# Router logits of the second expert layer computed by VectorE in some slots of the first expert layer

## The chip, the cores and the metric

One core of one Trainium2 chip runs the program. The metric is the device time of one execution in microseconds (us); the profile comes from one more execution, recorded by the hardware profiler.

## The reference

Three stages follow one another on 3,072 tokens of 512 numbers (fp32).

```python
x = attention(q, k, v, lam)                      # decayed linear attention, blocks of 64
# first expert layer: 8 experts, each token goes to one
e = argmax(x @ w_gate + modality_bias[modality_id])
x1 = gate_w * (relu(x @ w1[e]) @ w2[e])          # w1 512x1024, w2 1024x512
# second expert layer: a skip score and a second router decide
do = x1 @ w_skip > 0                             # w_skip: 512
logits = x1 @ w_gate2                            # w_gate2: 512 x 8
e2 = argmax(logits)                              # gate = 1 / sum(exp(logits - max))
out = x1 + do * gate2 * (relu(x1 @ w1b[e2]) @ w2b[e2])
```

The inputs are drawn with a fixed seed. For them the first layer's experts 0 to 7 get 0, 0, 0, 1319, 0, 253, 1494 and 6 tokens.

## The kernel before

**Slots.** Each expert layer works through slots of up to 256 tokens of one expert. A table kernel (`table`) on VectorE orders the experts from the fullest on and cuts their tokens into slots. For the inputs above the first layer has 14 slots: expert 6 in slots 0 to 5, expert 7 in slot 6 (6 tokens), expert 3 in slots 7 to 12 (39 tokens in the last), expert 5 in slot 13. A slot with at most 128 tokens is run as a half slot (`layer1_half`), by a flag `full` that every engine loads into a register one slot ahead; the flag comes from row 3 of `ei`. A slot that begins a new expert splits that expert's weights into a high and a low part on ScalarE and VectorE: `split_w2` at the slot's start, `split_w1` already in the layer 2 of the slot before (`split_next`).

**One slot** (`slot`) runs: layer 1 (eight column blocks f of w1, 12 matmuls of 256 columns each, hidden values to `p1`; after each second f ScalarE writes relu to `hh`, VectorE the rest to `hl`), then `trans_x` (eight transposes of the next slot's rows into `xth` and `xtl`, double-buffered by slot parity), then layer 2 for the two halves of the tokens (24 matmuls of 512 columns each into `p2[j]`). ScalarE scales the result into `x2r[parity][j]`; it is written to `xs2` and to the output.

**The router of the second layer** works one slot behind, in the layer 1 of the next slot (`router`): `tr` after f = 1 (eight TensorE transposes of `x2r`, copied by ScalarE to `x2t`), `la` after f = 3 (the products with `wgp`, 9 columns padded to 32, into `plg`), `rk` after f = 4 on VectorE (a transpose of `plg` into `L`, then argmax, the skip mask and the running counts `rs`), and `rb` in layer 2 (j = 0) after its fourth step: two small matmuls for the row numbers, eight small VectorE instructions, an Exp on ScalarE and two scatters by GpSimd into the second layer's table.

**Order.** The order of each engine's instructions is the order in which they are written out (`manual_schedule`). Inside an If, every engine that has work in it branches on its own register. All VectorE instructions count on one semaphore, and so do TensorE's and ScalarE's; an instruction that overwrites what the one before on its engine wrote waits for that one.

Of the kernel before, what the change touches and what calls it, by code (L numbers as in the profile page):

```python
# [9 lines left out]
F32 = mybir.dt.float32  # L10
# [4 lines left out]
AF = mybir.ActivationFunctionType  # L15
ALU = mybir.AluOpType
# [18 lines left out]
@with_exitstack  # L35
def body(ctx: ExitStack, tc: tile.TileContext, qkv, cpk, w1, w2, out, dbg=None):
    nc = tc.nc
# [150 lines left out]
    def choose(which, n):  # L188
        t = rt.tile([P, E], F32, tag="t_p", name="t_p")
        g = rt.tile([P, E], F32, tag="t_g", name="t_g")  # L190
        mx = rt.tile([P, 1], F32, tag="t_mx", name="t_mx")
        mp = rt.tile([P, 1], F32, tag="t_mp", name="t_mp")
        b = eb[:, which]
# [13 lines left out]
    def table(which):  # L207
        n = count(pcnt[which])
        x = rt.tile([P, KT, E], F32, tag="t_x", name="t_x")
        nr = rt.tile([P, E], F32, tag="t_nr", name="t_nr")  # L210
# [23 lines left out]

        u = rt.tile([P, E], F32, tag="t_u", name="t_u")
        y = rt.tile([P, KT], F32, tag="t_y", name="t_y")
        base = rt.tile([P, KT], F32, tag="t_b", name="t_b")
        nc.vector.scalar_tensor_tensor(out=u, in0=cc[:, 0:E], scalar=-float(T), in1=erow, op0=ALU.mult, op1=ALU.add)
# [5 lines left out]
        pick(eid, y)  # L244
        nx = rt.tile([P, E, E], F32, tag="t_nx", name="t_nx")
        nc.vector.tensor_tensor(out=nx, in0=bc(c1.unsqueeze(2), [P, E, E]), in1=bc(c1.unsqueeze(1), [P, E, E]), op=ALU.is_ge)
        nxe = rt.tile([P, E], F32, tag="t_nxe", name="t_nxe")
        nc.vector.tensor_reduce(out=nxe, in_=nx, axis=AX.X, op=ALU.add)
        w = rt.tile([P, KT], F32, tag="t_w", name="t_w")
        hx = rt.tile([P, KT], F32, tag="t_hx", name="t_hx")  # L250
        g2 = rt.tile([P, E], F32, tag="t_g2", name="t_g2")
        g3 = rt.tile([P, E], F32, tag="t_g3", name="t_g3")
        nc.vector.tensor_scalar(out=g2, in0=nxe, scalar1=estar, scalar2=None, op0=ALU.add)
# [5 lines left out]
        fin = ge[:, :, E - 1]  # L259
        nw = rt.tile([P, KT - 1], F32, tag="t_nw", name="t_nw")  # L260
        if which:
# [10 lines left out]
        nc.vector.scalar_tensor_tensor(out=u, in0=cc[:, 0:E], scalar=float(T), in1=nr, op0=ALU.mult, op1=ALU.add)  # L272
        rem = rt.tile([P, KT], F32, tag="t_r", name="t_r")
# [48 lines left out]
    def is_full(ap):  # L322
        return nc.values_load(ap, engines=FE, min_val=0, max_val=1,
                              skip_runtime_bounds_check_because="it is a comparison's result")

# [335 lines left out]
    def router(ix, kk=None):  # L661
# [38 lines left out]

        return tr, la, rk, rb

    def layer1(kk, steps, lead=False):
        xh, xl = xth[kk % 2], xtl[kk % 2]
        for f in range(8):
            pt = p1[(f // 2) % 3]
# [16 lines left out]
    def layer1_half(kk, steps):  # L723
        fs_ = [steps[f] for f in sorted(steps)]
        xh, xl = xth[kk % 2], xtl[kk % 2]
        for g in range(2):
            o = p1[g].rearrange("p a t -> p (a t)")
            fs = slice(g * 512, (g + 1) * 512)
            for c in range(4):
                nc.tensor.matmul(o, xh[:, c, 0:P], w1h[c][:, fs], start=(c == 0), stop=False)  # L730
                nc.tensor.matmul(o, xl[:, c, 0:P], w1h[c][:, fs], start=False, stop=False)
                nc.tensor.matmul(o, xh[:, c, 0:P], w1l[c][:, fs], start=False, stop=(c == 3))
            nc.scalar.activation(out=hrow[g], in_=o.rearrange("p (a f) -> p a f", f=P), func=AF.Relu)
            if g < len(fs_):
                fs_[g]()
# [41 lines left out]
    def first1():  # L777
# [35 lines left out]
    def first2():  # L813
        la, rk, rb = router(itl)[1:]

# [22 lines left out]
    def slots(which):  # L838
# [10 lines left out]
        def slot(kk, fl, full):  # L849
# [22 lines left out]
            if which == 0:  # L872
                tr, la, rk, rb = router(it[(kk - 1) % 6], kk - 1)
# [4 lines left out]
            with tc.If(full > 0, preferred_fallthrough_block=True) as c:  # L878
                layer1(kk, steps)
            with c.Else():  # L880
                layer1_half(kk, {} if which else {1: steps[1], 3: lambda: (la(), rk())})
# [93 lines left out]
```

## Time and profile before

| | |
|---|---|
| times of three runs | 704.35, 704.1, 699.21 us; median 704.1 |
| profiled execution, its own time | 700.19 us |
| its span | 698.5 us |
| TensorE busy in the span | 670.4 us (96%) |
| VectorE busy | 361.3 us (52%) |
| mean granted clock of TensorE | 0.996 |

The span is what the trace covers; the other 1.7 us of the profiled execution lie around it. Times in the rows are us from the span's start, unless marked ns. L713 is line 713 of the kernel.

### The profile page before, as it was taken

To read this page: it belongs to the slowest core of one execution; us is meant where nothing else is said; L and a number is where in the kernel's file an instruction comes from. 1 tells how busy PE (TensorE), PEld (TensorE's weight loads), DVE (VectorE), ACT (ScalarE), POOL (GpSimd) and SP (SyncE) were. 2 spreads that over 40 slices of the span, in tenths; PEclk is the share of its full clock that TensorE was granted. 3 is DMA by queue.
4 is the path that set the end of the run, shared out by engine and by line. 5 is a ranking of instruction groups with operands and counts; after the bars stand their busy time and mean duration, and the time that the engine had idled before them with its cause. 6 is when DMAs were issued, how large, how long until landed. Compare 5 with 4: busy or idle time off the path is not lost. (4 is left out here: it accounts for less than half of the span.)

```text
span 698.5 us, 16309 instructions
## 1 busy us (share of the span) xinstructions
PE 670.4 (96%) x5628; PEld 596.3 (85%) x5628; DVE 361.3 (52%) x920; ACT 262.4 (38%) x462; POOL 222.5 (32%) x287
## 2 busy tenths in 40 slices
PE   6999999899999999999999999999999999999994
PEld 5889988779988988799889887987998899887993
DVE  5656676663223315862233236868227575758650
ACT  2444434522222224832222226532115543556430
POOL 4356556252231132432311313234121222113221
PEclk9999999999999999999999999999999999999998
DMA  8778767647321232993211201631815558557500
GB/s 279 228 207 225 212 208 212 213 117 279 123 89 56 68 122 60 306 328 125 80 38 43 92 33 63 207 138 49 298 61 178 185 207 281 189 184 275 176 17 29
DMA packets 60504, 109.65 MB, mean 157 GB/s; under 512 B 18656, under 2 KB 18784, under 8 KB 60368
## 3 DMA queue, kind: packets, MB, share of 16 engines
q1 hardware_dynamic: 48400, 86.65, 38.0%
q0 software_dynamic: 9744, 20.47, 8.7%
q10 hardware_dynamic: 2224, 0.93, 0.6%
q8 instruction: 60, 0.98, 0.6%
q14 instruction: 76, 0.62, 0.3%
HBM read 84.08 MB, written 30.06 MB: 163 GB/s over the span
## 5 line engine op out<-in xcount | busy, mean ns | idle before, releaser
L713 PE MATMUL p<-xth,w1h 128*128 128x256 f32 x672 | 190.1, 283 | 4.2 <-ACTq L887 1.8
L713 PE MATMUL p<-xth,w1l 128*128 128x256 f32 x672 | 187.0, 278 | 0.0
L713 PE MATMUL p<-xtl,w1h 128*128 128x256 f32 x672 | 186.8, 279 | 0.0
L719 DVE SCALAR_TENSOR_TENSOR hl<-p,hh 128x512 fp32r<-128x512 f32 x84 | 57.7, 690 | 177.8 <-ACT hh L718 176.1
L752 PE MATMUL p<-w2h,hh 128*128 128x512 f32 x360 | 144.3, 401 | 0.0
L754 PE MATMUL p<-w2h,hl 128*128 128x512 f32 x360 | 141.5, 393 | 0.6 <-DVE hl L743 0.6
L753 PE MATMUL p<-w2l,hh 128*128 128x512 f32 x360 | 141.3, 392 | 0.4 <-DVE w2l L311 0.2
L713 PEld LDWEIGHTS p<-xth,w1h 128*128 128x128 f32 x672 | 126.2, 188 | 7.7 <-ACTq L887 2.3
L713 PEld LDWEIGHTS p<-xtl,w1h 128*128 128x128 f32 x672 | 126.2, 188 | 1.1 <-DVEq L772 0.5
L713 PEld LDWEIGHTS p<-xth,w1l 128*128 128x128 f32 x672 | 127.1, 189 | 0.0
L718 ACT ACTIVATE hh<-p 128x512 fp32r<-128x512 f32 x84 | 50.2, 598 | 184.1 <-PE p L713 182.0
L161 POOL DMA_INDIRECT out_dram<-x2r,it x43 | 50.4, 1171 | 199.7 <-DVE x2r L765 97.6
L754 PEld LDWEIGHTS p<-w2h,hl 128*128 128x128 f32 x360 | 67.6, 188 | 16.3 <-DVE hl L743 1.5
L753 PEld LDWEIGHTS p<-w2l,hh 128*128 128x128 f32 x360 | 67.7, 188 | 15.6 <-DVE w2l L311 2.4
L752 PEld LDWEIGHTS p<-w2h,hh 128*128 128x128 f32 x360 | 67.7, 188 | 13.0
L161 POOL DMA_INDIRECT tab<-pk,rows x28 | 32.0, 1143 | 143.7 <-issue 120.8
L165 POOL DMA_INDIRECT xg<-xs,it x54 | 60.2, 1115 | 28.7 <-issue 18.8
L311 DVE TENSOR_TENSOR w2l<-raw,w2h 128x1024 fp32r<-128x1024 f32 x48 | 55.9, 1219 | 6.8 <-ACT w2h L310 5.9
L762 ACT ACTIVATE x2r<-p,it 128x512 f32<-128x512 f32 x26 | 17.9, 688 | 106.8 <-PE p L754 92.3
L310 ACT CAST w2h<-raw 128x1024 fp32r<-128x1024 f32 x48 | 49.1, 1048 | 22.2 <-issue 12.5
L305 DVE TENSOR_TENSOR w1l<-raw,w1h 128x512 fp32r<-128x512 f32 x88 | 54.0, 686 | 0.9 <-issue 0.4
L304 ACT CAST w1h<-raw 128x512 fp32r<-128x512 f32 x88 | 47.0, 637 | 0.0
(214 smaller groups left out, 798.2 us busy)
## 6 DMA issues: line engine op xcount, KB each, us to landing
raw<-in_w_dram SPq DMA_DIRECT2D x96, 512.0 KB, 5.2
kq<-in_qkv_dram SPq DMA_DIRECT2D x48, 256.0 KB, 3.4
xs<-x2r SPq DMA_DIRECT2D x28, 256.0 KB, 2.6
v<-in_qkv_dram SPq DMA_DIRECT2D x24, 256.0 KB
xs<-xr SPq DMA_DIRECT2D x24, 256.0 KB, 6.1
xs<-xgm SPq DMA_DIRECT2D x7, 512.0 KB
xg<-xs,it POOLq DMA_INDIRECT x54, 4.7
tab<-tini ACTq DMA_DIRECT2D x2, 416.0 KB
```

The lines of the kernel that those rows point to most:

```text
L161: nc.gpsimd.indirect_dma_start(out=dst, out_offset=bass.IndirectOffsetOnAxis(ap=idx, axis=0), in_=rows, in_offset=None, bounds_check=dst.s ...
L165: return nc.gpsimd.indirect_dma_start(out=rows, out_offset=None, in_=src, in_offset=bass.IndirectOffsetOnAxis(ap=idx, axis=0), bounds_chec ...
L304: nc.scalar.copy(out=w1h[c][:, s], in_=raw1[:, c, s])
L305: nc.vector.tensor_tensor(out=w1l[c][:, s], in0=raw1[:, c, s], in1=f32(w1h[c][:, s]), op=ALU.subtract)
L310: nc.scalar.copy(out=w2h[c], in_=r)
L311: nc.vector.tensor_tensor(out=w2l[c], in0=r, in1=f32(w2h[c]), op=ALU.subtract)
L713: nc.tensor.matmul(o, w[c][:, fs], x[:, c, :], start=(n == 0), stop=(n == 11))
L718: nc.scalar.activation(out=a, in_=pt, func=AF.Relu)
L719: nc.vector.scalar_tensor_tensor(out=b, in0=pt, scalar=0.0, in1=f32(a), op0=ALU.max, op1=ALU.subtract)
L752: nc.tensor.matmul(p2[j], a, w2h[g][:, i], start=(n == 0), stop=False)
L753: nc.tensor.matmul(p2[j], a, w2l[g][:, i], start=False, stop=False)
L754: nc.tensor.matmul(p2[j], b, w2h[g][:, i], start=False, stop=(n == 7))
```

## The change

In slots 2 to 10 of the first layer, layer 1 is cut into three Ifs (f = 0 and 1; f = 2 and 3; f = 4 to 7). The flag of the first layer becomes 2 where the slot is full and neither it nor the next one begins a new expert. Where it is 2, VectorE computes the 9 logits for the 2 times 128 tokens of the slot before, with 18 instructions `tensor_tensor_reduce`: each multiplies `x2r[..][j]` (128x512) by one row of `wgb` and sums along the row into one column of `L`. The products, which nobody reads, go to `xtl` of the slot before. `wgb` holds the 9 weight rows on every partition; SP loads it once, in `first1`, between the loads of w1 and w2. 11 of the 18 stand ahead of layer 1, 3 ahead of f = 2 and 4 behind f = 3. Where the flag is less, `tr`, `la` and the transpose of `plg` (`turn`) stay, at the same places of layer 1. In all slots 2 to 10 `rk` stands behind the last `hl`, the `hl` of f = 4 to 7 is written in two instructions of 256 columns, and `rb` stands after the seventh step of layer 2 (j = 0), and so behind `split_next`. Slots 1 and 11 to 13 keep the old order. The small tiles of `table` and `choose` get one buffer in place of two.

```diff
-        nc.vector.tensor_scalar(out=ei_[:, 3 * KT:4 * KT], in0=rem, scalar1=float(P), scalar2=None, op0=ALU.is_gt)
+        if which:
+            nc.vector.tensor_scalar(out=ei_[:, 3 * KT:4 * KT], in0=rem, scalar1=float(P), scalar2=None, op0=ALU.is_gt)
+        else:
+            nc.vector.tensor_tensor(out=w[:, 0:KT - 2], in0=nw[:, 0:KT - 2], in1=nw[:, 1:KT - 1], op=ALU.max)
+            nc.vector.tensor_scalar(out=w[:, 0:KT - 2], in0=w[:, 0:KT - 2], scalar1=-1.0, scalar2=2.0, op0=ALU.mult, op1=ALU.add)
+            nc.vector.scalar_tensor_tensor(out=ei_[:, 3 * KT + 1:4 * KT - 1], in0=rem[:, 1:KT - 1], scalar=float(P),
+                                           in1=w[:, 0:KT - 2], op0=ALU.is_gt, op1=ALU.mult)
...
+    wgb = hp.tile([P, E + 1, D], F32, name="wgb")
...
+        def lg(j, es):
+            for e in es:
+                nc.vector.tensor_tensor_reduce(
+                    out=xtl[kk % 2][:, :, j * P:(j + 1) * P], in0=x2r[kk % 2][j].rearrange("p (c t) -> p c t", t=P),
+                    in1=wgb[:, e].rearrange("p (c t) -> p c t", t=P), scale=1.0, scalar=0.0, op0=ALU.mult, op1=ALU.add,
+                    accum_out=box["L"][:, j, e:e + 1])
+
+        def turn():
+            if "L" not in box:
+                box["L"] = rt.tile([P, 2, 32], F32, tag="L2", name="L2", bufs=1)
+            nc.vector.transpose(out=box["L"].rearrange("p j e -> p (j e)"), in_=plg)
+
         def rk():
-            L = rt.tile([P, 2, 32], F32, tag="L2", name="L2")
-            nc.vector.transpose(out=L.rearrange("p j e -> p (j e)"), in_=plg)
+            if "L" not in box:
+                turn()
+            L = box.pop("L")
...
-                nc.vector.scalar_tensor_tensor(out=b, in0=pt, scalar=0.0, in1=f32(a), op0=ALU.max, op1=ALU.subtract)
+                for q in range(parts):
+                    q_ = slice(q * 2 // parts, (q + 1) * 2 // parts)
+                    nc.vector.scalar_tensor_tensor(out=b[:, q_], in0=pt[:, q_], scalar=0.0, in1=f32(a[:, q_]), op0=ALU.max, op1=ALU.subtract)
...
         behind(ld_w1(e), got)
+        nc.sync.dma_start(out=wgb, in_=bc(wgr.unsqueeze(0), [P, E + 1, D]))
         ld_w2(e)
...
+            if which == 0 and 2 <= kk <= 10:
+                box["L"] = rt.tile([P, 2, 32], F32, tag="L2", name="L2", bufs=1)
+                own = nc.values_load(ei[0][0:1, 3 * KT + kk:3 * KT + kk + 1], engines=(ET.DVE,), min_val=0, max_val=2,
+                                     skip_runtime_bounds_check_because="it comes from comparisons' results")
+                with tc.If(own > 1):
+                    lg(0, range(E + 1))
+                    lg(1, range(0, 2))
+                with tc.If(full > 0, preferred_fallthrough_block=True) as c:
+                    layer1(kk, {}, (0, 1))
+                with c.Else():
+                    half_rows(kk, 0)
+                with tc.If(full > 1, preferred_fallthrough_block=True) as c:
+                    lg(1, range(2, 5))
+                    layer1(kk, {}, (2, 3))
+                    lg(1, range(5, E + 1))
+                with c.Else():
+                    with tc.If(full > 0, preferred_fallthrough_block=True) as c2:
+                        steps[1]()
+                        layer1(kk, {}, (2, 3))
+                        la()
+                        turn()
+                    with c2.Else():
+                        steps[1]()
+                        half_rows(kk, 1)
+                        la()
+                        turn()
+                with tc.If(full > 0, preferred_fallthrough_block=True) as c:
+                    layer1(kk, {}, range(4, 8), parts=2)
+                with c.Else():
+                    half_cols()
+                rk()
+            else:
+                with tc.If(full > 0, preferred_fallthrough_block=True) as c:
+                    layer1(kk, steps)
+                with c.Else():
+                    layer1_half(kk, {} if which else {1: steps[1], 3: lambda: (la(), rk())})
             trans_x(which, kk + 1, ptr)
             hooks = {1: ahead, 5: lambda: split_next(which, kk + 1, fl2)}
             if which == 0:
-                hooks[3] = rb
+                hooks[6 if 2 <= kk <= 10 else 3] = rb
```

`half_rows(kk, g)` and `half_cols()` are the two loops of the old `layer1_half`, cut out as functions.

## Rows read from the trace of the kernel before

**Rows 1.** The page's part 1: busy us of each engine, share, instructions.

```profile
PE 670.4 (96%) x5628; PEld 596.3 (85%) x5628; DVE 361.3 (52%) x920; ACT 262.4 (38%) x462; POOL 222.5 (32%) x287
```

**Rows 2.** Who waited for whom: us in total, times, longest us.

```profile
ACT hh L718 <- PE p L713: 182.0, 78, 13.2
DVE hl L719 <- ACT hh L718: 176.1, 64, 10.6
```

**Rows 3.** Timeline of TensorE in slot 2: start us, us, line, operation, tiles.

```profile
178.90 0.28 PE L713 MATMUL p<-xth,w1h 128*128 128x256 f32 x1
...
181.53 0.28 PE L713 MATMUL p<-xth,w1l 128*128 128x256 f32 x1
...
182.64 0.28 PE L713 MATMUL p<-xtl,w1h 128*128 128x256 f32 x1
...
185.23 0.28 PE L713 MATMUL p<-xth,w1l 128*128 128x256 f32 x1
...
186.25 0.28 PE L713 MATMUL p<-xtl,w1h 128*128 128x256 f32 x1
...
191.47 0.28 PE L713 MATMUL p<-xth,w1l 128*128 128x256 f32 x1
...
195.22 0.18 PE L137 MATMUL pmi<-oh,tri 128*128 128x16 bf16 x1
...
203.63 0.28 PE L713 MATMUL p<-xth,w1h 128*128 128x256 f32 x1
```

**Rows 4.** Timeline of VectorE in slot 2.

```profile
186.95 0.13 DVE L681 CAST idf<-it 128x2 f32<-128x2 int32 x1
...
188.63 0.36 DVE L133 TENSOR_TENSOR rs<-rs,oh 128x8 bf16<-128x8 bf16 x2
...
192.42 0.69 DVE L719 SCALAR_TENSOR_TENSOR hl<-p,hh 128x512 fp32r<-128x512 f32 x1 [1.97 <-ACT hh L718]
...
195.47 0.17 DVE L141 COPY rs<-rs 128x8 bf16<-128x8 bf16 x1 [1.16 <-PE pmi L138]
...
196.50 0.17 DVE L158 RECIPROCAL pk<-s 128x2 f32<-128x2 f32 x1
```

**Rows 5.** Branch instructions of layer 1's If (L878), 194 to 206 us: ns, start.

```profile
L878 DVEq COMPARE_BRANCH  x1: 50/50/50, 198.2 to 198.2; - x1
```

**Rows 6.** Register loads (L323) of VectorE in the same stretch: ns, start.

```profile
L323 DVEq TENSOR_LOAD <-ei x1: 311/311/311, 197.8 to 197.8; - x1
```

**Rows 7.** Groups by form: busy us, mean ns, idle before.

```profile
L305 DVE TENSOR_TENSOR w1l<-raw,w1h 128x512 fp32r<-128x512 f32 x88 | 54.0, 686 | 0.9 <-issue 0.4 <-ACT w1h L304 0.3
...
L133 DVE TENSOR_TENSOR rs<-rs,oh 128x8 bf16<-128x8 bf16 x52 | 8.5, 163 | 1.8
...
L743 DVE TENSOR_TENSOR hl<-p,hh 128x256 fp32r<-128x256 f32 x12 | 4.3, 417 | 1.5 <-ACT hh L740 1.5
...
L455 DVE TENSOR_TENSOR_SCAN dm<-lad,diag 128x512 f32<-128x512 f32 x2 | 2.4, 1224 | 0.1
...
L233 DVE TENSOR_REDUCE t_r<-t_x 128x24 f32<-128x192 f32 x2 | 0.7, 354 | 0.1
```

**Rows 8.** Timeline of VectorE in slot 5: a run of splits.

```profile
271.08 4.91 DVE L305 TENSOR_TENSOR w1l<-raw,w1h 128x512 fp32r<-128x512 f32 x8 [0.16 <-issue]
```

**Rows 9.** Branch instructions of L878, 182 to 194 us (end of slot 2's layer 1).

```profile
L878 PEldq COMPARE_BRANCH  x1: 305/305/305, 189.6 to 189.6; - x1
```

**Rows 10.** Timeline of TensorE where half slot 6 skips its second half.

```profile
292.71 0.40 PE L754 MATMUL p<-w2h,hl 128*128 128x512 f32 x1
293.84 0.38 PE L713 MATMUL p<-xth,w1h 128*128 128x256 f32 x1 [0.73 <-ACTq L887]
```

**Rows 11.** A stretch of slot 1: busy us by engine, clock, DMA share, GB/s.

```profile
155.00:160.00 5.00, 5.00 (x45) 5.00 (x44) 0.69 (x1) 1.56 (x3) 0.23 (x1) 1.00 0.96 323
```

**Rows 12.** Timeline of SP's queue behind the load of w1.

```profile
167.95 0.40 SPq L335 DMA_DIRECT2D it<-tab  x1
```

**Rows 13.** Timeline of GpSimd in slot 2.

```profile
197.47 1.09 POOL L161 DMA_INDIRECT tab<-pk,rows  x1 [13.39 <-issue]
```

More of the change, by code (lines that the diff above doesn't have):

```diff
@@ L35, in body @@
 @with_exitstack
-def body(ctx: ExitStack, tc: tile.TileContext, qkv, cpk, w1, w2, out, dbg=None):
+def body(ctx: ExitStack, tc: tile.TileContext, qkv, cpk, w1, w2, wgr, out, dbg=None):
     nc = tc.nc
@@ L188, in choose @@
     def choose(which, n):
[L189 to L192, printed above, removed]
+        t = rt.tile([P, E], F32, tag="t_p", name="t_p", bufs=1)
+        g = rt.tile([P, E], F32, tag="t_g", name="t_g", bufs=1)
+        mx = rt.tile([P, 1], F32, tag="t_mx", name="t_mx", bufs=1)
+        mp = rt.tile([P, 1], F32, tag="t_mp", name="t_mp", bufs=1)
         b = eb[:, which]
@@ L233, in pick @@
             nc.vector.tensor_reduce(out=out, in_=x, axis=AX.X, op=ALU.add)
-        u = rt.tile([P, E], F32, tag="t_u", name="t_u")
-        y = rt.tile([P, KT], F32, tag="t_y", name="t_y")
-        base = rt.tile([P, KT], F32, tag="t_b", name="t_b")
+        u = rt.tile([P, E], F32, tag="t_u", name="t_u", bufs=1)
+        y = rt.tile([P, KT], F32, tag="t_y", name="t_y", bufs=1)
+        base = rt.tile([P, KT], F32, tag="t_b", name="t_b", bufs=1)
         nc.vector.scalar_tensor_tensor(out=u, in0=cc[:, 0:E], scalar=-float(T), in1=erow, op0=ALU.mult, op1=ALU.add)
@@ L244, in table @@
         pick(eid, y)
-        nx = rt.tile([P, E, E], F32, tag="t_nx", name="t_nx")
+        nx = rt.tile([P, E, E], F32, tag="t_nx", name="t_nx", bufs=1)
         nc.vector.tensor_tensor(out=nx, in0=bc(c1.unsqueeze(2), [P, E, E]), in1=bc(c1.unsqueeze(1), [P, E, E]), op=ALU.is_ge)
-        nxe = rt.tile([P, E], F32, tag="t_nxe", name="t_nxe")
+        nxe = rt.tile([P, E], F32, tag="t_nxe", name="t_nxe", bufs=1)
         nc.vector.tensor_reduce(out=nxe, in_=nx, axis=AX.X, op=ALU.add)
[L249 to L252, printed above, removed]
+        w = rt.tile([P, KT], F32, tag="t_w", name="t_w", bufs=1)
+        hx = rt.tile([P, KT], F32, tag="t_hx", name="t_hx", bufs=1)
+        g2 = rt.tile([P, E], F32, tag="t_g2", name="t_g2", bufs=1)
+        g3 = rt.tile([P, E], F32, tag="t_g3", name="t_g3", bufs=1)
         nc.vector.tensor_scalar(out=g2, in0=nxe, scalar1=estar, scalar2=None, op0=ALU.add)
@@ L259, in table @@
         fin = ge[:, :, E - 1]
-        nw = rt.tile([P, KT - 1], F32, tag="t_nw", name="t_nw")
+        nw = rt.tile([P, KT - 1], F32, tag="t_nw", name="t_nw", bufs=1)
         if which:
@@ L322, in is_full @@
     def is_full(ap):
-        return nc.values_load(ap, engines=FE, min_val=0, max_val=1,
-                              skip_runtime_bounds_check_because="it is a comparison's result")
+        return nc.values_load(ap, engines=FE, min_val=0, max_val=2,
+                              skip_runtime_bounds_check_because="it comes from comparisons' results")
     def XG(which, kk):
@@ L699, in rb, with layer1 @@
                 scatter(tabv[1][j], pk[:, j, :], rows[:, j:j + 1])
-        return tr, la, rk, rb
-    def layer1(kk, steps, lead=False):
+        return tr, la, rk, rb, lg, turn
+    def layer1(kk, steps, fr=range(8), lead=False, parts=1):
         xh, xl = xth[kk % 2], xtl[kk % 2]
-        for f in range(8):
+        for f in fr:
             pt = p1[(f // 2) % 3]
@@ L718, in layer1, with half_rows, half_cols @@
                 nc.scalar.activation(out=a, in_=pt, func=AF.Relu)
-                nc.vector.scalar_tensor_tensor(out=b, in0=pt, scalar=0.0, in1=f32(a), op0=ALU.max, op1=ALU.subtract)
+                for q in range(parts):
+                    q_ = slice(q * 2 // parts, (q + 1) * 2 // parts)
+                    nc.vector.scalar_tensor_tensor(out=b[:, q_], in0=pt[:, q_], scalar=0.0, in1=f32(a[:, q_]), op0=ALU.max, op1=ALU.subtract)
             if f in steps:
                 steps[f]()
-    def layer1_half(kk, steps):
-        fs_ = [steps[f] for f in sorted(steps)]
+    def half_rows(kk, g):
         xh, xl = xth[kk % 2], xtl[kk % 2]
[L726 to L735, printed above, removed]
+        o = p1[g].rearrange("p a t -> p (a t)")
+        fs = slice(g * 512, (g + 1) * 512)
+        for c in range(4):
+            nc.tensor.matmul(o, xh[:, c, 0:P], w1h[c][:, fs], start=(c == 0), stop=False)
+            nc.tensor.matmul(o, xl[:, c, 0:P], w1h[c][:, fs], start=False, stop=False)
+            nc.tensor.matmul(o, xh[:, c, 0:P], w1l[c][:, fs], start=False, stop=(c == 3))
+        nc.scalar.activation(out=hrow[g], in_=o.rearrange("p (a f) -> p a f", f=P), func=AF.Relu)
+    def half_cols():
         for g in range(2):
@@ L743, in layer1_half @@
                 nc.vector.tensor_tensor(out=hl[g][:, as_, 0:P], in0=pt[:, as_], in1=f32(hh[g][:, as_, 0:P]), op=ALU.subtract)
+    def layer1_half(kk, steps):
+        fs_ = [steps[f] for f in sorted(steps)]
+        for g in range(2):
+            half_rows(kk, g)
+            if g < len(fs_):
+                fs_[g]()
+        half_cols()
         for st_ in fs_[2:]:
@@ L813, in first2 @@
     def first2():
-        la, rk, rb = router(itl)[1:]
+        la, rk, rb = router(itl)[1:4]
         tb = table(1)
@@ L876, in slot @@
             full2 = is_full(ei[which][0:1, 3 * KT + kk + 1:3 * KT + kk + 2])
[L878 to L881, printed above, removed]
+            if which == 0 and 2 <= kk <= 10:
+                box["L"] = rt.tile([P, 2, 32], F32, tag="L2", name="L2", bufs=1)
+                own = nc.values_load(ei[0][0:1, 3 * KT + kk:3 * KT + kk + 1], engines=(ET.DVE,), min_val=0, max_val=2,
+                                     skip_runtime_bounds_check_because="it comes from comparisons' results")
+                with tc.If(own > 1):
[23 more added lines that the diff above has]
+                with c.Else():
+                    half_cols()
+                rk()
[4 more added lines that the diff above has]
+                    layer1_half(kk, {} if which else {1: steps[1], 3: lambda: (la(), rk())})
             trans_x(which, kk + 1, ptr)
@@ L920, in body @@
         dbg(nc, locals())
-_INS = ["qkv", "cpk", "w1", "w2"]
+_INS = ["qkv", "cpk", "w1", "w2", "wgr"]
 _OUTS = [((3072, 512), "float32")]
@@ L957 @@
         _np.ascontiguousarray(ids).view(_np.float32)], axis=1)
+    inputs["wgr"] = _np.concatenate([_np.asarray(inputs[n]).reshape(hd, -1) for n in ("moe2_w_gate", "moe2_w_skip")], axis=1).T
     inputs["w1"] = _np.concatenate([inputs["moe_w1"], inputs["moe2_w1"]], axis=0)
```

20 lines of the change are left out of this document (10 added, 10 removed).

## The prediction

> **What bounds the kernel now.** I read the busy times first: TensorE works in 96% of the span, VectorE in 52% [rows 1]. Then the list of waits: the longest are ScalarE waiting for TensorE's hidden values and VectorE waiting for ScalarE behind it, 182 and 176 us [rows 2]. So the other engines wait for TensorE, not it for them. Then the timeline of TensorE through one slot: it issues without a gap from 178.90 to the next slot's first matmul at 203.63, one slot in 24.73 us [rows 3]. In that stage anything taken off TensorE shortens the program one for one, as long as nothing else becomes late. Read VectorE's timeline of the same slot for what it has left: some 10 us of small work, the rest idle [rows 2, 4].
>
> **In how many slots.** The flag is 2 where the slot is full, is not the first of its expert, and the next slot is not either. With the slots that the token counts give (expert 6 in 0 to 5, expert 7 in 6, expert 3 in 7 to 12), within 2 to 10 these are 2, 3, 4 and 8, 9, 10: six slots, in two runs of three. Slots 5, 6 and 7 take the other branches.
>
> **What is removed, per slot.** From the last layer-1 matmul ahead of the transposes to the second behind them it is 182.64 - 181.53 = 1.11 us; two steps in the undisturbed layer 1 take 2 x 0.115 = 0.23 (from 186.25 to 191.47 there are 46 steps: 0.1135 each; from 182.64 to 185.23 22: 0.118). So `tr` costs TensorE 1.11 - 0.23 = 0.88. In the same way `la`: 186.25 - 185.23 - 0.23 = 0.79 [rows 3]. Together 1.67 us; six slots: **10.0 us**. Two copies of ScalarE and VectorE's transpose go too; neither is waited for here.
>
> **What VectorE gets, per slot.** 18 sums. No row shows this instruction, so let s be the time from one start to the next, and see how large s may be. VectorE's queue of one slot, in the new order: 18 s; two `hl` of 512 columns at 0.69 + 0.03 [rows 4]; two pairs of 256 columns, at 0.417 each and overlapped [rows 7], 0.80 a pair; `rk` without the transpose, from 186.95 to the end of L133 at 188.99, 2.04 [rows 4]. That is 18 s + 5.1. It begins after `rb`: its first VectorE instruction starts 0.25 behind the small matmul (195.22 to 195.47), the last ends 1.20 later (196.67) [rows 3, 4]; then the branches and register loads until layer 1's branch at 198.25 take 1.6 [rows 5], and the load of `own` with its branch I put at 0.4 more, for such a load takes 0.311 [rows 6] and a branch 0.050 [rows 5]. So the sums start 3.45 us behind the matmul of `rb`, and `rk` has to be done when the next slot's `rb` comes, one slot of 24.73 - 1.67 = 23.06 later, for TensorE stands still there until `oh` is ready. 18 s + 5.1 + 3.45 <= 23.06 gives **s <= 0.806**. Each 0.01 above costs 0.18 us a slot, and at s = 0.90 the 1.67 are gone. All other needs are looser: `p1` of f = 0 is wanted again at f = 6, layer 2 wants the last `hl` 20 matmuls in.
>
> **Which s.** The bounds are 0.60 below (eight subtractions of the same 128x512, both operands in SBUF, in 4.91: 0.60 from start to start [rows 8]) and 1.26 above (the scan over two streams of 512 takes 1224 ns [rows 7], and 0.04 for a wait). The multiplication alone takes 686 ns, and a reduction of 192 elements 354, as much above its length as the others have: summing goes at the same rate there [rows 7]. All sums of one j write the same part of `xtl`, so each waits for the one before; such a wait adds 0.04 (L133 twice in 0.36 at 0.163 each [rows 4, 7]): 0.73. If the sum is written out by a small instruction of its own, overlapped like the subtractions, it is 0.60 + 0.16 + 0.04 = 0.80. I take 0.77, nearest to the plain 686 ns row, and so no loss; but the margin is 0.04. [...]
>
> **The rest.** The three Ifs: TensorE's own branch at the end of layer 1 runs at 189.6, while the matmuls last until 191.6 [rows 3, 9]. The sequencer is 2 us ahead, and a branch takes 0.3, so two more are hidden; uncovered they would cost some 0.4 each. That nothing stands still at today's block ends: behind 191.47 the transposes and layer 2 follow (TensorE has no gap until 195.22) though VectorE's `hl` of the block only starts at 192.42 [rows 3, 4]. `rb` moves behind nine more matmuls of 0.23: GpSimd's scatter starts 2.1 us later; GpSimd has waited 13.39 us for it [rows 13], and what is queued behind (the output scatters, the gathers for the slot after next) has a slot to spare. In slots 5 and 6 `rb` also stands behind `split_next`, 4.91 us of VectorE [rows 8] and as much of ScalarE (for the Exp); `split_w2` comes 1.4 later in slot 7, and layer 2 reads it 13 us on. Nothing. In half slot 6 `hl` no longer waits behind `rk`: at most 0.4 gained. `wgb` is 128 x 18,432 bytes, 2.36 MB, behind w1 on SP's queue. At the 323 GB/s of that stretch it takes 7.3 us; the load of w2 and the DMA of the table at 167.95 come that much later [rows 11, 12]. w2 is split five slots later. The first sums of slot 2 need `wgb` at about 175; if it comes later than that, one slot loses up to some 3 us, which I put at 0. Changes of buffer counts in `table`: one engine in order, 0.
>
> **The sum.** 700.19 - 10.0 = 690.2 by the profiled execution; 704.1 - 10.0 = 694.1 by the median, 3.9 above it. The three runs lie on both levels; I take the middle and a little: **692.5**.
>
> **Rivals.** (1) VectorE becomes the bound by a little: s between 0.84 and 1.0. For it: the margin is thin, and every fixed cost counts 18 times. Against: 0.73 and 0.80 both fit. At 0.92 a slot loses 18 x 0.114 = 2.05 against 1.67: 2 us slower, 696 to 706. (2) The sums run at half rate: s = 1.26 from the scan's 1224 ns [rows 7]. A slot then loses 18 x 0.454 = 8.2, less 1.67 is 6.5; six slots 39: **slower**, about 740. It decides from s = 0.90 on. Against it: the scan feeds a product back, the reduction's row does not show two cycles. [...] (3) The new blocks make TensorE stop: where half slot 6 skips a block, the next matmul starts 1.13 behind the last one in place of 0.23: 0.90 lost [rows 10]. One such stop in each of the six slots leaves 6 x 0.77 = 4.6 of gain: about 699. Against: the block skipped there holds all TensorE work of its If; in the new Ifs each branch has matmuls. (4) The flag is never 2, or in one slot only: then nothing is gained, 704.
>
> **How the numbers follow.** Forecast 0.55 (its own range 688 to 696), rival 1 0.16, rival 2 0.12, rival 3 0.13, rival 4 0.04. A measurement of this kernel tells 1% from no change, 7 us. Faster by over 1%: the forecast and a third of rival 1, 0.60. Within 1%: rivals 3 and 4 and some of rival 1, 0.24. Slower: rival 2 and the slow end of rival 1, 0.16. The range reaches from 687 (the profiled level, with the small gains) to 712 (rival 1 up to s = 0.97); outside it lie rival 2 and little else.
>
> **What would show it.** In slots 2, 3, 4 the first layer-1 matmuls should stand 23.06 apart (24.73 now), with no transposes of `x2r` and no L674 there; L667 loses 48 of its matmuls. 108 sums at 0.69 to 0.76 us. No wait of TensorE at the small matmul of `rb` (L137): a wait there on `oh` is rival 1, and 8 us of it rival 2. A gap behind f = 1 or f = 3 is rival 3. VectorE's busy time rises by 108 x 0.7 = 76 us. Wrong it would be by s over 0.9, or by a wait of the first sum for something later than `x2r[..][0]`: if it started only when the second half is done, 4 us later than I let it, the slot would lose about that much.

## The result and the profile after

| | before | changed |
|---|---|---|
| times, median of 6 | 703.26 us (699.21 to 704.35) | 692.01 us (691.07 to 695.14) |
| profiled execution, its span | 700.19, 698.5 us | 692.02, 690.2 us |
| mean granted clock of TensorE | 0.996 | 0.993 |

The ratio of the times is 0.9855, interval 0.9824 to 0.9887: some 10 us faster. The forecast was 692.5.

The page's part 1, to be read against [rows 1]: VectorE has 72 us more, TensorE 10.0 less.

```profile
PE 660.4 (96%) x5388; PEld 588.2 (85%) x5388; DVE 433.2 (63%) x1148; ACT 256.9 (37%) x450; POOL 223.5 (32%) x287
```

TensorE's timeline of slot 3 of the changed kernel: start, us, line, operation, tiles. It answers to [rows 3] (L733 was L713, L780 to L782 were L752 to L754).

```profile
205.28 0.28 PE L733 MATMUL p<-xth,w1h 128*128 128x256 f32 x1
...
216.06 0.28 PE L733 MATMUL p<-xth,w1l 128*128 128x256 f32 x1
216.18 1.03 PE L356 MATMUL ptr<-ident,xg 128*128 128x128 f32 x8
216.97 0.48 PE L780 MATMUL p<-w2h,hh 128*128 128x512 f32 x1
217.29 0.40 PE L781 MATMUL p<-w2l,hh 128*128 128x512 f32 x1
217.52 0.39 PE L782 MATMUL p<-w2h,hl 128*128 128x512 f32 x1
...
221.88 0.18 PE L137 MATMUL pmi<-oh,tri 128*128 128x16 bf16 x1
...
228.23 0.28 PE L733 MATMUL p<-xth,w1h 128*128 128x256 f32 x1
```

From 205.28 to 228.23 the slot takes 22.95 us, where it took 24.73. Between the first and the last matmul of layer 1 lie 95 steps in 10.78 us, 0.1135 each, with nothing between them: no stop behind f = 1 or f = 3, at the new branches. Of the six slots only slot 2 is longer, 23.26: a step of 0.22 behind f = 3, and a slower pace (0.118) from there on.

VectorE's timeline of the same slot: the first sums, then the end of its queue in that slot.

```profile
202.47 0.69 DVE L686 CUSTOM_DVE_ANT_0 xtl<-x2r,wgb 128x512 fp32r<-128x512 f32 x1 [2.08 <-issue]
203.09 0.08 DVE L686 DVE_READ_ACCUMULATOR2_ANT L<- 128x1 f32 x1
203.20 0.69 DVE L686 CUSTOM_DVE_ANT_0 xtl<-x2r,wgb 128x512 fp32r<-128x512 f32 x1
203.82 0.08 DVE L686 DVE_READ_ACCUMULATOR2_ANT L<- 128x1 f32 x1
203.94 0.69 DVE L686 CUSTOM_DVE_ANT_0 xtl<-x2r,wgb 128x512 fp32r<-128x512 f32 x1
...
216.41 1.41 DVE L741 SCALAR_TENSOR_TENSOR hl<-p,hh 128x256 fp32r<-128x256 f32 x4
...
219.46 0.36 DVE L133 TENSOR_TENSOR rs<-rs,oh 128x8 bf16<-128x8 bf16 x2
```

A sum is two instructions, the product with its sum (0.69) and a read of the accumulator (0.08); from one sum to the next it is 0.735. Two distances are to be read between this fence and the one above. The ranking ends at 219.82, 2.06 ahead of the small matmul of `rb` (L137, 221.88). The first half of `hl` for f = 4 and 5 ends about 0.42 after 216.41 (a lone 256-column `hl` takes 0.417, [rows 7]), at 216.83; the third matmul of layer 2, the first that reads `hl`, starts at 217.52, 0.69 later. In slots 4, 8, 9 and 10 the same distance is 0.65, 0.72, 0.50 and 0.50; in slot 2, whose sums start earlier, 2.24.

Slot by slot, from first matmul of layer 1 to the next, worked out from the two timelines of TensorE:

| stretch | before | changed | difference |
|---|---|---|---|
| start to slot 0 | 124.65 | 126.81 | +2.16 |
| slot 0 | 29.28 | 30.25 | +0.97 |
| slot 1 | 24.97 | 24.96 | -0.01 |
| slots 2, 3, 4, 8, 9, 10 | 148.42 | 138.04 | -10.38 |
| slots 5, 6, 7 | 65.58 | 65.26 | -0.32 |
| slots 11, 12, 13 | 69.69 | 70.49 | +0.80 |
| second layer and end | 235.91 | 234.39 | -1.52 |

The six slots give the forecast's 10 us; the other rows take 2.1 back, and the span is 8.3 shorter. Most of that is the start, where the change moves no work. Ahead of slot 0 TensorE waited 2.41 us (0.69 before) for ScalarE's copy of the last attention output, which ScalarE itself began late, 1.24 us after it had become free; for what, the trace doesn't say (it prints `remote`). Timelines of the changed kernel, ScalarE, then TensorE:

```profile
126.17 0.58 ACT L547 COPY xt<-psO 128x512 f32<-128x512 f32 x1 [1.24 <-remote]
```

```profile
126.81 0.38 PE L733 MATMUL p<-xth,w1h 128*128 128x256 f32 x1 [2.41 <-ACT xt L547]
```

Behind that wait the granted clock was 0.80 and then 0.50, where it was 1.00 before the change. The views by stretch, before, then changed (the last three numbers are clock, DMA share and GB/s):

```profile
128.00:130.00 2.00, 2.00 (x20) 2.00 (x19) 1.19 (x2) 1.42 (x4) 0.00 (x0) 1.00 1.11 374
```

```profile
126.00:128.00 2.00, 1.19 (x7) 1.19 (x8) 0.00 (x0) 0.58 (x1) 0.98 (x2) 0.80 1.06 400
128.00:130.00 2.00, 2.00 (x11) 1.90 (x10) 0.00 (x0) 0.00 (x0) 0.00 (x0) 0.50 1.18 306
```

In a second profile of the changed kernel (e10, below) the clock stays at 1.00 there and slot 0 takes 28.90, so the change doesn't always bring the fall. Whether it makes it likelier isn't shown: of the kernel before there is one profile only. Slot 0's start is no steadier: over the profiles of the changed kernel and its variants below it lies between 123.46 and 126.81. The second layer's 1.5 comes back in the last section.

### The profile page after: what moved, and what is told of

Same layout as the page of the kernel before. It is cut to its first block, busy times and chain, and to the rows that moved or that the text cites. A ratio compares the mean times of both kernels' runs of the same rounds, so it can differ in the third digit from the quotient of the medians.

```text
span 690.2 us, 16306 instructions
## 1 busy us (share of the span) xinstructions
PE 660.4 (96%) x5388; PEld 588.2 (85%) x5388; DVE 433.2 (63%) x1148; ACT 256.9 (37%) x450; POOL 223.5 (32%) x287
## 5 line engine op out<-in xcount | busy, mean ns | idle before, releaser
L733 PE MATMUL p<-xth,w1h 128*128 128x256 f32 x672 | 189.1, 282 | 6.0 <-ACT xt L547 2.4
L733 PE MATMUL p<-xth,w1l 128*128 128x256 f32 x672 | 187.1, 279 | 0.0
L733 PE MATMUL p<-xtl,w1h 128*128 128x256 f32 x672 | 186.8, 279 | 0.0
L780 PE MATMUL p<-w2h,hh 128*128 128x512 f32 x360 | 144.6, 402 | 0.0
L782 PE MATMUL p<-w2h,hl 128*128 128x512 f32 x360 | 141.6, 393 | 0.3 <-DVE hl L763 0.3
L733 PEld LDWEIGHTS p<-xth,w1h 128*128 128x128 f32 x672 | 126.7, 189 | 9.2 <-ACT xt L547 2.7
L733 PEld LDWEIGHTS p<-xtl,w1h 128*128 128x128 f32 x672 | 126.8, 189 | 1.1 <-issue 0.2
L733 PEld LDWEIGHTS p<-xth,w1l 128*128 128x128 f32 x672 | 126.9, 189 | 0.0
L741 DVE SCALAR_TENSOR_TENSOR hl<-p,hh 128x512 fp32r<-128x512 f32 (+1 forms) x100 | 58.1, 601 | 81.0 <-ACT hh L738 71.3
L686 DVE CUSTOM_DVE_ANT_0 xtl<-x2r,wgb 128x512 fp32r<-128x512 f32 x108 | 74.2, 691 | 15.4 <-issue 8.0
L782 PEld LDWEIGHTS p<-w2h,hl 128*128 128x128 f32 x360 | 67.7, 188 | 15.8 <-DVE hl L763 0.9
L161 POOL DMA_INDIRECT tab<-pk,rows x28 | 33.6, 1199 | 140.6 <-issue 117.6
L780 PEld LDWEIGHTS p<-w2h,hh 128*128 128x128 f32 x360 | 67.8, 188 | 12.7
```

What stands on the lines that cost most here:

```text
L161: nc.gpsimd.indirect_dma_start(out=dst, out_offset=bass.IndirectOffsetOnAxis(ap=idx, axis=0), in_=rows, in_offset=None, bounds_check=dst.s ...
L686: nc.vector.tensor_tensor_reduce(out=xtl[kk % 2][:, :, j * P:(j + 1) * P], in0=x2r[kk % 2][j].rearrange("p (c t) -> p c t", t=P), in1=wgb[ ...
L733: nc.tensor.matmul(o, w[c][:, fs], x[:, c, :], start=(n == 0), stop=(n == 11))
L741: nc.vector.scalar_tensor_tensor(out=b[:, q_], in0=pt[:, q_], scalar=0.0, in1=f32(a[:, q_]), op0=ALU.max, op1=ALU.subtract)
L780: nc.tensor.matmul(p2[j], a, w2h[g][:, i], start=(n == 0), stop=False)
L782: nc.tensor.matmul(p2[j], b, w2h[g][:, i], start=False, stop=(n == 7))
```

## Experiments

Each was run beside the kernel before on the same chip; the ratio is to that. It isn't the quotient of the two medians in the table. The kernel before has medians from 700.46 to 706.07 in these groups, so a time in us is compared within its group only; apart from e2, e3 and e8, whose theories fell, four medians lie outside what was expected in us (e5 and e7 by 0.2 above, e9 by 2.4 and e10 by 1.4 below).

| run | median us | before | ratio (interval) |
|---|---|---|---|
| e1 order only | 703.57 | 706.07 | 0.9988 (0.9962 to 1.0013) |
| e2 two more sums | 697.35 | 706.07 | 0.9905 (0.9870 to 0.9941) |
| e3 six more sums | 725.37 | 706.07 | 1.0291 (1.0253 to 1.0328) |
| e4 other form | 691.01 | 706.07 | 0.9802 (0.9760 to 0.9845) |
| e5 two dumps, two more | 693.21 | 704.43 | 0.9859 (0.9817 to 0.9901) |
| e6 two more behind hl | 692.95 | 704.43 | 0.9847 (0.9809 to 0.9885) |
| e7 rb at 3 | 693.18 | 704.43 | 0.9851 (0.9812 to 0.9889) |
| e8 slots 1 to 11 | 700.20 | 704.43 | 0.9944 (0.9916 to 0.9972) |
| e9 slot 5 too | 687.63 | 700.46 | 0.9803 (0.9768 to 0.9838) |
| e10 changed kernel | 689.63 | 700.46 | 0.9831 (0.9796 to 0.9865) |

**e1: the order alone.**

```diff
-            ... in0=w[:, 0:KT - 2], scalar1=-1.0, scalar2=2.0, op0=ALU.mult, op1=ALU.add)
+            ... in0=w[:, 0:KT - 2], scalar1=0.0, scalar2=1.0, op0=ALU.mult, op1=ALU.add)
```

> Everything of the change but the sums: the flag is held at 1, so all slots 2 to 10 keep the transposes and the products on TensorE; the three Ifs, the later ranking, the later rb, the halved hl and the load of wgb stay. Theory (the gain is the TensorE time of tr and la and nothing else): slots 2, 3, 4, 8, 9, 10 are back at 24.7 to 24.95 us (22.95 with the sums), no stop behind f = 1 and f = 3, time 701 to 705, as before (703.3). Rival (the new order itself gains): these slots below 24.4, time 698 or less. Rival (the blocks cost): each of the slots 25.3 or more, time above 706.

The time is that of before. Four of the six slots take 24.77 to 24.80; TensorE's timeline shows slot 9 from its first matmul to the next slot's:

```profile
345.05 0.28 PE L733 MATMUL p<-xth,w1h 128*128 128x256 f32 x1
...
369.84 0.28 PE L733 MATMUL p<-xth,w1h 128*128 128x256 f32 x1
```

Slots 3 and 4 took 25.88 and 25.32 in that profile, with stops of TensorE at `la`. Blocks, later ranking, later `rb`, halved `hl` and the load of `wgb` gain nothing and cost at most 0.08 a slot, apart from such stops. The gain is TensorE's work that the sums replace.

**e2 and e3: how much room VectorE has.** `lg` gets an offset `at` into the columns of `L`; e3 has 6 for 2.

```diff
                     lg(1, range(5, E + 1))
+                    lg(1, range(0, 2), E + 1)
```

> Two more sums in each of the six slots, behind the last four, into columns of L that nobody reads; all else as in the changed kernel. Theory (VectorE has room: in the trace after, rk ends 1.87 to 2.12 us ahead of the small matmul of rb, and two sums take 1.47): slots stay at 22.95, slack falls to about 0.5, time 691 to 693. By the prediction's own budget (18 s + 5.1 + 3.45 against 23.06, 1.28 left at s = 0.735) 0.2 us a slot would be lost: 693.2. Rival (VectorE already sets the pace somewhere): 1.47 a slot, 701.

> Six more sums in each of the six slots, behind the last four, into columns of L that nobody reads. Theory (VectorE becomes the bound once the slack of about 2.0 us is used up): six sums take 4.41, so each slot grows by 2.3 to 2.4 us to about 25.3, six slots 14 us, time 706; TensorE waits at the small matmul of rb (L137). By the prediction's budget 4.41 - 1.28 = 3.1 a slot, 711. Rival (VectorE's work in layer 1 is hidden whatever it is): unchanged, 692.

e2 came out between its theory and its rival, e3 far above both, so the theory had the wrong place. The list of TensorE's waits names another than L137; e2, then e3 (us in total, times, longest):

```profile
PE p L782 <- DVE hl L741: 4.4, 5, 1.1
```

```profile
PE p L782 <- DVE hl L741: 20.6, 6, 4.1
```

The timelines of e2 in slot 4, TensorE then VectorE, show which `hl` it is:

```profile
238.04 0.39 PE L781 MATMUL p<-w2l,hh 128*128 128x512 f32 x1
239.54 0.51 PE L782 MATMUL p<-w2h,hl 128*128 128x512 f32 x1 [1.11 <-DVE hl L741]
```

```profile
238.45 0.69 DVE L686 CUSTOM_DVE_ANT_0 xtl<-x2r,wgb 128x512 fp32r<-128x512 f32 x1
239.07 1.41 DVE L741 SCALAR_TENSOR_TENSOR hl<-p,hh 128x256 fp32r<-128x256 f32 x4
```

The third matmul of layer 2 reads the `hl` of f = 0, which was written long before. But it starts only when the first of the four halves of f = 4 to 7 is done: 239.07 + 0.42 = 239.49. The reason, by the code: the third If has another branch, `half_cols`, whose first VectorE instruction writes that same part of `hl`; one wait has to serve both branches, and it counts VectorE's instructions, so it falls on the first of the block in either. This reason is read from the code; no run takes the other branch away. What the timelines show is that the matmul starts 0.05 behind that half in all five slots that wait. Every sum behind f = 3 thus stands ahead of layer 2. There were 0.69 us of room; two sums take 1.47, and 0.78 should be lost: the five waits are 0.68 to 1.11 (slot 2 has none, its sums start earlier). The six slots together are 5.5 us longer than in the changed kernel, 143.53 against 138.04; by the two ratios the time is 3.5 longer.

In e3 the waits make 20.6 us, the six slots 34.1 more. Behind the waits the matmuls also run slower for a while: in the timelines of slots 2, 3, 8 and 9 they start 0.43 apart there in place of 0.23, some 7 us in all. In slot 3 the granted clock fell with it, as the view by stretch shows:

```profile
218.00:221.00 3.00, 0.28 (x2) 0.00 (x0) 2.86 (x9) 0.53 (x2) 0.00 (x0) 1.00 0.00 0
221.00:224.00 3.00, 1.65 (x4) 1.36 (x5) 2.86 (x13) 0.00 (x0) 0.00 (x0) 0.54 0.02 5
224.00:227.00 3.00, 3.00 (x8) 2.32 (x8) 2.27 (x9) 0.21 (x1) 0.00 (x0) 0.50 0.00 0
```

TensorE stands still for 4.1 us and the granted clock falls from 1.00 to 0.50. In slot 2, where it stood 1.91, the matmuls from 194.09 to 197.08 start 0.43 apart as well; in e2's slot 4, behind 1.11, they start 0.23 apart from 239.88 to 243.79.

**e4: the other form of the sum,** the prediction's rival 2.

```diff
-                nc.vector.tensor_tensor_reduce(out=..., in0=..., in1=..., scale=1.0, scalar=0.0, op0=ALU.mult, op1=ALU.add,
+                nc.vector.scalar_tensor_tensor(out=..., in0=..., scalar=1.0, in1=..., op0=ALU.mult, op1=ALU.mult,
                     accum_out=...)
```

> The 18 sums are written as scalar_tensor_tensor with an accumulator (times 1.0, times the weight row) in place of tensor_tensor_reduce; operands, order and results as in the changed kernel. Rival 2 of the prediction (the fused form with two fp32 sources in SBUF runs at half rate): one such instruction takes about 1.22 us, 18 of them 9.5 more, less 2.0 of slack 7.4 a slot, time about 736. Theory (a sum costs no more than a plain product, here as there): 0.69 each and the time of the changed kernel, 692.

The groups by form (busy, mean ns), e4, then the changed kernel:

```profile
L686 DVE SCALAR_TENSOR_TENSOR xtl<-x2r,wgb 128x512 fp32r<-128x512 f32 x108 | 74.2, 691 | 15.2 <-issue 9.9 <-ACT x2r L790 2.4
```

```profile
L686 DVE CUSTOM_DVE_ANT_0 xtl<-x2r,wgb 128x512 fp32r<-128x512 f32 x108 | 74.2, 691 | 15.4 <-issue 8.0 <-ACT x2r L790 2.4 <-DMA xs<-x2r 2.1
...
L686 DVE DVE_READ_ACCUMULATOR2_ANT L<- 128x1 f32 x108 | 8.8, 82 | 0.0
```

Both forms take 691 ns; a plain subtraction of that size with both sources in SBUF takes 686 ([rows 7]; the prediction calls it a product). Two fp32 sources in SBUF and an accumulator thus take 5 ns more than the two sources alone, in either form, and not the 1.22 us of the rival. The sum is written out by a second instruction in both, 82 ns here and 81 in e4.

**e5 and e6: the room by place, and what a wait costs.** e5 is e2 with a second dump; e6 is the changed kernel with the two sums elsewhere.

```diff
-                    out=xtl[kk % 2][:, :, j * P:(j + 1) * P], in0=x2r...
+                    out=xtl[kk % 2][:, :, (e % 2) * P:(e % 2 + 1) * P], in0=x2r...
```

```diff
                     half_cols()
+                with tc.If(own > 1):
+                    lg(1, range(0, 2), E + 1)
                 rk()
```

> The kernel of e2 (two more sums), but sums with an odd e dump into the second half of xtl and those with an even e into the first, so that none overwrites what the one before it wrote. Theory (each sum now waits for the write of the one before, 0.735 from start to start where 0.62 would do; and e2 was slow because the sums push the first hl of f = 4 behind the third matmul of layer 2): sums start 0.62 apart, 20 of them take less than the 18 did, the wait of L782 on hl is gone, slots 22.95, time 691 to 693 against 697 in e2. Rival (0.735 is the instruction with its read of the accumulator, no wait): 0.735 stays, time 697.

> The same two more sums as in e2, but in an If of VectorE's own behind the last hl, ahead of the ranking. Theory (what has least room is hl, not the ranking: hl of f = 4 is 0.7 us ahead of the matmul of layer 2 that waits for it, the ranking 2.0 us ahead of rb): 1.47 and a branch of about 0.3 fit in the 2.0, slots 22.95 to 23.1, time 691 to 693.5. Rival (the amount of VectorE work is what counts, wherever it stands): as e2, slots 24.1, time 697.

VectorE's timeline of e5, sums of slot 3:

```profile
202.37 0.68 DVE L686 CUSTOM_DVE_ANT_0 xtl<-x2r,wgb 128x512 fp32r<-128x512 f32 x1
202.98 0.08 DVE L686 DVE_READ_ACCUMULATOR2_ANT L<- 128x1 f32 x1
202.98 0.68 DVE L686 CUSTOM_DVE_ANT_0 xtl<-x2r,wgb 128x512 fp32r<-128x512 f32 x1
```

Without the overwritten dump a sum starts 0.61 behind the last one, as the plain subtractions do ([rows 8]), and the read of the accumulator runs beside the next. So the wait on the predecessor's write costs 0.12 of the 0.735. Twenty sums then take no longer than eighteen did (with two `hl` 13.89 in e5's slot 4, less a wait of 1.10 for ScalarE, against 13.94 in the changed kernel's), and the time is back: ratio 0.9859 against 0.9905 in e2. e6 keeps 0.735 and the two sums of e2, but behind `hl`: 0.9847. Both intervals overlap that of e2, so it is the slots that decide: 23.92 to 24.33 in the five of e2 that wait at L782, while five of six in e5 take 22.94 to 22.99, and e6's slots 2, 8 and 9 take 22.95 or 22.96. TensorE's and VectorE's timelines of e6, slot 3:

```profile
216.61 0.18 PE L137 MATMUL pmi<-oh,tri 128*128 128x16 bf16 x1
```

```profile
216.05 0.36 DVE L133 TENSOR_TENSOR rs<-rs,oh 128x8 bf16<-128x8 bf16 x2
```

Its ranking ends 0.2 ahead of `rb` here and in slots 4, 9 and 10, so that room is used up. The place counts, not the amount: `hl` had 0.69 of room, the ranking 2.06.

The slots that stay longer have another late engine. In e5 slot 4 takes 23.92: ScalarE's relu of f = 2 and 3 starts 1.85 late, at 232.56 where slot 3's distance from one relu to the next (205.02 to 207.77) asks for 230.71, VectorE's `hl` waits for it in order, and L782 0.70 for that. In e6 slots 3, 4 and 10 take 23.17, 23.63 and 23.39; there, too, that relu is late and L782 starts 0.1 to 0.6 later than its place asks.

**e7: was the later rb needed?**

```diff
-                hooks[6 if 2 <= kk <= 10 else 3] = rb
+                hooks[3] = rb
```

> rb is put back behind the fourth step of layer 2 in slots 2 to 10; all else as in the changed kernel. Theory: rb comes 2.1 us earlier, but so do its VectorE instructions and with them the next sums (by about 1.1, then x2r sets their start); rk is then about 1.1 ahead of rb, hl of f = 4 about 1.9 ahead of layer 2: no stop, slots 22.95, time 691 to 693. Rival (the later rb is what lets the ranking stand behind the last hl): TensorE waits at L137 for oh, up to 0.3 us a slot, 692 to 694, and more where a wait drops the clock.

All six slots take 22.94 to 22.99, and the ratio is that of the changed kernel (0.9851, 0.9855). But not with the room that I expected. TensorE's and VectorE's timelines of slot 3:

```profile
218.03 0.18 PE L137 MATMUL pmi<-oh,tri 128*128 128x16 bf16 x1
```

```profile
217.61 0.36 DVE L133 TENSOR_TENSOR rs<-rs,oh 128x8 bf16<-128x8 bf16 x2
```

The ranking ends at 217.97, 0.06 ahead; TensorE keeps its pace. The sums do start 1.2 earlier, but the ranking stands behind the last `hl`, and that follows TensorE's last matmul of layer 1, not the sums. The move of `rb` bought spare room that this kernel doesn't use.

Half slot 6 took 19.42 in that profile (15.46 in the changed kernel's). TensorE waited there for ScalarE, which came over 2 us late to `half_cols`, and behind it the granted clock was 0.57 (286 to 290; 1.00 in the stretches before and after), the matmuls from 286.74 to 289.30 0.43 apart:

```profile
284.71 1.07 ACT L760 CAST hh<-p 128x512 fp32r<-128x512 f32 x2 [3.31 <-remote]
```

```profile
285.35 0.50 PE L780 MATMUL p<-w2h,hh 128*128 128x512 f32 x1 [2.16 <-ACT hh L760]
```

The trace doesn't name what ScalarE waited for. e9 below has `rb` at the same place and takes 15.67 there, so it isn't shown to come from the move.

**e8 and e9: two tries at more.** e8:

```diff
+            nc.sync.dma_start(out=wgb, ...)          # in slot 0, in late(), and no longer between w1 and w2
-            if which == 0 and 2 <= kk <= 10:
+            if which == 0 and 1 <= kk <= 11:
-                hooks[6 if 2 <= kk <= 10 else 3] = rb
+                hooks[6 if 1 <= kk <= 11 else 3] = rb
+                out=xtl[kk % 2][:, :, (e % 2) * P:(e % 2 + 1) * P]     # as in e5
```

> A try at more: the sums with two dump halves, wgb loaded in slot 0 behind the last rows (SP's queue is idle there from 131 on) and no longer between w1 and w2, and the new order in slots 1 to 11, so that slots 1 and 11 take the sums as well. Theory (1.67 to 1.79 us of TensorE for every slot that takes them, and VectorE has room for choose in slot 11): eight slots in place of six, time 688 to 689.5. Rival (slot 1 or 11 has no room on VectorE, or the load of wgb holds up the rows of slot 1): 691 or more.

The theory fell: slot 1 took 28.14 in place of 24.96, slot 11 29.74 in place of 24.93. Timelines of slot 11, VectorE, then TensorE:

```profile
395.52 0.69 DVE L686 CUSTOM_DVE_ANT_0 xtl<-x2r,wgb 128x512 fp32r<-128x512 f32 x1 [1.80 <-ACT hh L738]
...
402.50 0.69 DVE L741 SCALAR_TENSOR_TENSOR hl<-p,hh 128x512 fp32r<-128x512 f32 x1
```

```profile
403.33 0.55 PE L733 MATMUL p<-xth,w1h 128*128 128x256 f32 x1 [3.27 <-DVE hl L741]
```

In slot 11 `choose` stands ahead of the sums on VectorE and waits for a matmul at the slot's start (391.33), so the sums begin 4.2 us into layer 1; in slot 3 they began 2.8 before it. The `hl` of f = 0 and 1 stands behind eleven of them, f = 6 needs the buffer that it reads, and behind the wait of 3.27 the granted clock is 0.65 (401 to 406, with the wait in it) and 0.66 (406 to 411), where it was 1.00 until 401. In slot 1, too, the sums begin 2.8 after layer 1 (158.46 against 155.66). TensorE loses 2.74 there, but before it comes to f = 6:

```profile
166.03 0.38 PE L733 MATMUL p<-xtl,w1h 128*128 128x256 f32 x1 [2.74 <-issue]
```

This is the second matmul of f = 5, which needs nothing of that `hl`, and the trace names no releaser; nor does it for 1.87 us in the midst of f = 4 in slot 4. By my estimate, 12 steps of 0.118 behind the first matmul of f = 5 (163.01), f = 6 would have come at about 164.4 without the stop and waited for that `hl`, which ends at 166.14; so slot 1 has no room either, but only slot 11 shows it.

e9 leaves slots 1 and 11 alone and takes slot 5:

```diff
-            ... in0=nw[:, 0:KT - 2], in1=nw[:, 1:KT - 1], op=ALU.max)
+            ... in0=nw[:, 0:KT - 2], in1=nw[:, 0:KT - 2], op=ALU.max)
-                hooks[6 if 2 <= kk <= 10 else 3] = rb
+                hooks[3] = rb
+                out=xtl[kk % 2][:, :, (e % 2) * P:(e % 2 + 1) * P]     # as in e5
```

> A second try at more, with what e5 and e7 left room for: sums with two dump halves, rb behind the fourth step, and the flag 2 also where the next slot begins a new expert, so that slot 5 takes the sums as well (seven slots; slots 1 and 11 stay as they were, which e8 showed to have no room). Theory: slot 5 goes from 24.9 to about 23.0, its split of w1 starts no later than in e7, time 1.8 below the changed kernel run beside it: 690 to 691. Rival (slot 5's ranking comes late, rb and the splits behind it too, and slot 6 starts late): slot 5 and 6 together no shorter, 692 or more.

> The changed kernel itself once more, beside e9 and the kernel before, for a second profile. Theory (six slots at 22.95, the rest as before up to the wait for the rows of slot 0 and stops behind branches): 691 to 693, slots 2 to 4 and 8 to 10 within 0.3 of 22.95.

Slot 5 takes 23.07 (24.96 in e10), and the median is 2.0 below the changed kernel beside it, as expected; but the intervals of the two ratios overlap, so it is not shown to be faster. Its profile also shows what may take the gain away: in slot 7 TensorE waits for the copies of ScalarE, which stands in the splits of w2 behind their load (a wait of 2.48 ahead of the one at 290.08), and the slot took 29.16 for 24.86.

```profile
296.72 1.01 PE L681 MATMUL pmi<-x2t,wgp 128*32 128x64 f32 x32 [2.49 <-ACT x2t L675]
```

In e10 the six slots take 23.27 (slot 2) and 22.95 to 22.98, as in the first profile.

## Why the prediction was right, and where it was not

- **The slots.** Six, as counted: L667 had 104 transposes into `ptr`, L674 (the same line now) has 56, 48 less; 108 sums.
- **The 1.67 a slot: 1.78 measured in slot 3** (24.73 to 22.95; 1.73 on average, for slot 2 took 23.26). The missing 0.11 is the pace of f = 2 and 3. Behind `tr` the steps took 0.118 ([rows 3]); without it all run at 0.1135 (not in slot 2), and 24 steps give 0.11. e1, which puts `tr` and `la` back, gives 24.77 to 24.80 again.
- **s: 0.735 measured, 0.77 taken.** The low sum, 0.69 and 0.04 for a wait, gave the number by an error that cancelled: the next sum could start at 0.61, and the wait costs 0.12 (e5). That is luck in the working, not in the choice: 0.735 lies between the two values weighed. No run shows the 0.80: the small instruction that it counts at 0.16 takes 0.08, and in e5 it runs beside the next sum.
- **"All other needs are looser": wrong.** This is the step that failed, without harm to the time. The tightest need is not the ranking ahead of `rb` but the first `hl` of the last block ahead of the third matmul of layer 2, where the text had the last `hl`, 20 matmuls in. The ranking's budget of 18 s + 5.1 + 3.45 allowed s up to 0.806 and gave 1.28 us to spare at 0.735; the trace shows 2.06 there, for some sums wait for no predecessor's write (18 sums and two `hl` take 13.94 from 202.47 to 216.41, where 18 x 0.735 + 1.44 gives 14.67). `hl` has 0.69 left, so s could be 0.735 + 0.69 / 18 = 0.773 (0.763 by the 0.50 of slots 9 and 10). Two more sums, which the budget priced at 0.2 a slot, cost 0.9 (e2), and six, which it priced at 3.1, 5.7 (e3). With the 0.80 that I held possible there would have been a loss by this, some 0.5 a slot, where the text let it pass (0.806). The other need that it called loose, `p1` of f = 0 at f = 6, is what stopped TensorE in e8's slot 11, where the sums began 7 us later.
- **Break-even at s = 0.90: too generous,** for the same reason: by `hl` it would be about 0.773 + 1.78 / 18 = 0.87, an estimate, and lower if the matmuls slow down too, as they did behind waits of 1.9 to 4.1 us (e3: 0.43 apart in place of 0.23).
- **VectorE had more left than read:** it was busy 6.8 us in slot 2 before, not some 10; 18.8 in slot 3 of the changed kernel.
- **The later rb costs nothing: right,** and it wasn't needed either, by 0.05 to 0.07 us (e7). **wgb in time: right;** the first sum, at 177.44 in slot 2, followed ScalarE's `x2r`, not the load.
- **Rival 1** didn't come, by 0.03 to 0.04 in s. **Rival 2** fell in both forms (e4). **Rival 3:** no stop of TensorE at the blocks in the six slots of two profiles of the changed kernel, beyond a step of 0.2 in slot 2; e1 shows some in two slots, e7 one in half slot 6. **Rival 4** fell with the 108 sums.
- **Half slot 6: 0.57 gained** (16.03 to 15.46) where I said at most 0.4, but 0.17 in e10 (15.86). Slot 12, also a half slot, lost 0.9 to 1.1 behind its second matmul in both profiles of the changed kernel and in e1 to e6, and not in e7 to e9; the trace names now one, now another small instruction of `choose` as releaser, so its cause wasn't settled.
- **The level.** I took 692.5 between 690.2 and 694.1; the profiled execution had 692.02 only because 3.1 us up to slot 0's end and 0.8 in slots 11 to 13 were lost and 1.5 gained in the second layer; the six slots alone would have given 689.8. That the number came out within 0.5 is luck; the 10 us is not.

## What to carry to other kernels

Work moved to an idle engine was free here up to the first instruction behind it that the busy engine waits for: `hl` with 0.69 us of room, where the ranking had 2.06. Look for that one by place, in the queue and in the wait counts: here, by the code, a wait behind an If fell where both branches need it, two blocks later than the data. Then add a little work on purpose, in two places (e2 and e6): it tells which need is the tight one.

A scratch output that nobody reads still made each sum wait for the one before; two halves used in turn gave 0.12 us of 0.735 back (e5).

## What was not expected of the hardware

**Two paces of the same matmuls.** The 96 matmuls of a layer 1 run 0.1135 or 0.118 apart; in the slots read here the pace changes only where TensorE stopped or did other work, and then holds. In the second layer, whose slots have the same code in both kernels, a whole layer 1 takes 11.70 or 12.10. Changed kernel, slots 18 and 19, first matmul of layer 1 and of layer 2:

```profile
550.64 0.28 PE L733 MATMUL p<-xth,w1h 128*128 128x256 f32 x1
...
562.33 0.48 PE L780 MATMUL p<-w2h,hh 128*128 128x512 f32 x1
...
573.42 0.28 PE L733 MATMUL p<-xth,w1h 128*128 128x256 f32 x1
...
585.52 0.48 PE L780 MATMUL p<-w2h,hh 128*128 128x512 f32 x1
```

Of slots 16 to 20, four ran at the slow pace in the profile before and one in the changed kernel's; with slot 22 that makes the 1.6 us between them, and no run here says what sets it.

**Stops without a releaser.** Now and then an engine comes 0.5 to 2.7 us late to instructions in the new blocks: TensorE in e1 (slots 3 and 4, at `la`) and e8 (slots 1 and 4), ScalarE in e5 (slot 4) and e7 (slot 6), and in the changed kernel's first profile in slots 8 to 10 (its relu of f = 2 and 3, at no cost to TensorE). The trace names nothing that it waited for. ScalarE's late copy ahead of slot 0 (126.17, 1.24 late) is of the same kind, and no If stands ahead of it in the program, so what stops the engines stays open.
